# A linear-attention and adapter kernel: a new hand-written order of all instructions, an earlier gate for the stores, and a last slot finished in two halves

## The chip, the cores and the metric

The kernel runs on one core of one Trainium2 chip. The metric is device microseconds of one execution. A profiled execution has, beside its own time, a span: the time from the first to the last instruction of the program in the trace. The core has these engines, and each takes its instructions strictly from a list of its own: TensorE (PE, with its weight loads shown apart as PEld), VectorE (DVE), ScalarE (ACT), GpSimd (POOL) and SyncE (SP), which here only issues transfers.

## The reference, cut to what matters

```python
# q, k, v: (8, 8, 576, 64) float32: batch, heads, sequence, head dimension
r_q, r_k = relu(q), relu(k)
q_p = concat(r_q * cos_w, r_q * sin_w)        # cos_w, sin_w depend on the position alone
k_p = concat(r_k * cos_w, r_k * sin_w)
kv  = einsum('bhsf,bhsd->bhfd', k_p, v);  z = sum(k_p, axis=2)
x   = einsum('bhsf,bhfd->bhsd', q_p, kv) / (einsum('bhsf,bhf->bhs', q_p, z) + 1e-6)
x   = x.transpose(0, 2, 1, 3).reshape(4608, 512)

logits = x @ w_gate                           # 8 experts
top 2 of the logits, softmax over the two -> w
out = x + sum over the two experts e of  w_e * ((x @ A[e]) @ B[e])     # rank 16
```

The output is 4608 x 512 float32, 9.4 MB; q, k and v are 28 MB together.

## The kernel before, in words

**Batches and slots.** The eight batches are loaded one after another, each as three transfers, v, k and q, which also turn float32 into bf16 on the way (batch 0's v and k come as float32). The 4608 output rows are worked off in 36 slots of 128 rows. Nine slots belong to two batches; every ninth slot from 4 on is mixed, half its rows from each of the two. Slot n of 0 to 8 needs batches 0 and 1, 9 to 17 batches 2 and 3, and so on.

**One batch.** `vs` scales v by the cosine and by the sine of the position: 18 instructions (9 sequence parts, 2 tables), spread over ACT, POOL and, for the first batches, DVE. `rk` is the relu of k, `qc` of q, in two halves `qc,b,0` and `qc,b,1`, on DVE. `kv` is 72 small matmuls in three parts into the PSUM tile `big`; `kve` copies their sum to SBUF, in two halves.

**One slot.** `qt` transposes q on PE, `qe` multiplies by the tables (DVE). `nd` makes numerators and denominators on PE in the one PSUM tile `nd`; `re` is the reciprocal, `no` the quotient x (both DVE, both reading `nd`, so the next slot's `nd` waits for `no`). `xt` and `xe` transpose x by way of the PSUM tile `xz` and copy it, `za` multiplies it with the adapters' A and the gate's columns, `mx` takes the largest logits.

**One group of up to three slots** (`GROUPS`; the last one holds slot 35 alone). `nm` sums the two largest logits, `mk` marks the experts that are out, `tt` and `cb` make the sigmoid's argument, `sg` is the sigmoid (ACT), `zg` multiplies, `zt` transposes (into the other half of `xz`) and `ze` copies. A softmax over two logits is the sigmoid of their difference, so `tt` computes 2 * logit - sum, and `cb` pushes the others far down.

**Output of a slot.** `dx` adds x (turned into row order by a permutation matmul) and the adapters' product in a PSUM bank, `oe` copies it to one of 22 output buffers, `st` stores 256 KB by SP's queue.

**What sets the order.** Nothing is scheduled by a compiler: the string `ORDER` names every piece of work with its engine (`T` PE, `A` ACT, `V` DVE, `G` and `W` POOL, `S` SP) and its arguments, and each engine's list is the order in which its pieces stand there. An instruction waits for what it reads, and for the readers of what it overwrites; behind a waiting instruction its whole engine waits. `W` is a scaling on POOL that waits in addition for DVE's latest `vs`, `rk` or `qc`. `dm` are matmuls of ones without a use for the result, which keep PE running in waits; a further 36 stand at the start.

**The gate.** SP's list has, ahead of the first store, a tiny transfer `gate` that reads the q of batch 7 and so waits for its landing. The stores stand behind it:

```python
    def gate(e, b):
        e.dma_start(out=gone, in_=q_b[b % 5][0:1, 0, 0, 0:2])
```

Of the kernel before, what the change touches and what calls it, by code (L numbers as in the profile page):

```python
# [22 lines left out]
ldv,G,2,0 vs,A,0,0,1 vs,V,0,0,0 ldk,G,2,0 vs,V,0,1,0 vs,A,0,1,1 vs,V,0,3,0 vs,A,0,2,1 vs,V,0,3,1 ldq,G,2,0  # L23
vs,V,0,4,0 vs,A,0,2,0 vs,V,0,4,1 vs,A,0,5,0 ldv,G,3,0 vs,V,0,6,0 vs,V,0,6,1 vs,A,0,5,1 vs,V,0,7,1 vs,A,0,7,0
# [30 lines left out]
xt,T,17 oe,A,11 re,V,18 za,T,15 no,V,18 qt,T,20 ze,A,4 za,T,16 xe,A,17 dx,T,12,b0 qe,V,20 nd,T,19 oe,A,12
mx,V,15 mx,V,16 qc,V,5,0 xt,T,18 za,T,17 vs,W,6,0,0 vs,A,6,0,1 re,V,19 dx,T,13,b1 no,V,19 xe,A,18 vs,G,6,1,0
dx,T,14,b0 vs,A,6,3,0 mx,V,17 vs,G,6,1,1 rk,V,5,0 nd,T,20 oe,A,13 vs,W,6,2,0 xt,T,19 oe,A,14 qt,T,21 mk,V,5
nm,V,5 re,V,20 vs,G,6,2,1 xe,A,19 tt,V,5 no,V,20 kv,T,5,0 vs,G,6,3,1 vs,A,6,6,1 cb,V,5 kv,T,5,1 qe,V,21
vs,G,6,4,0 sg,A,5 vs,A,6,8,1 xt,T,20 vs,G,6,4,1 zg,V,5 kv,T,5,2 xe,A,20 vs,G,6,5,1 qc,V,5,1 nd,T,21 vs,W,6,5,0
kve,A,5,1 rk,V,6,0 zt,T,5 vs,W,6,6,0 za,T,18 kve,A,5,0 qt,T,22 za,T,19 ze,A,5 re,V,21 qt,T,23 qe,V,22 vs,G,6,7,0  # L60
dx,T,15,b0 vs,G,6,7,1 mx,V,18 mx,V,19 dx,T,17,b1 no,V,21 vs,G,6,8,0 za,T,20 qt,T,24 oe,A,15 qe,V,23 xt,T,21
nd,T,22 oe,A,17 mx,V,20 qe,V,24 xe,A,21 kv,T,6,0 mk,V,6 vs,G,7,0,1 vs,A,7,0,0 nm,V,6 re,V,22 qt,T,25 tt,V,6
no,V,22 vs,A,7,1,0 vs,G,7,2,0 kv,T,6,1 vs,A,7,1,1 vs,G,7,2,1 qt,T,26 cb,V,6 qe,V,25 sg,A,6 nd,T,23 vs,G,7,3,0
vs,A,7,3,1 zg,V,6 xt,T,22 vs,G,7,5,0 vs,A,7,4,0 kv,T,6,2 re,V,23 xe,A,22 vs,G,7,6,0 no,V,23 za,T,21 vs,G,7,8,0
kve,A,6,1 zt,T,6 mx,V,21 qe,V,26 nd,T,24 vs,G,7,8,1 ze,A,6 za,T,22 kve,A,6,0 qc,V,6,0 xt,T,23 mx,V,22 vs,A,7,4,1
re,V,24 dx,T,16,b0 no,V,24 xe,A,23 dx,T,18,b1 vs,A,7,5,1 qc,V,6,1 za,T,23 nd,T,25 oe,A,16 rk,V,7,0 gate,S,7
# [43 lines left out]
def kernel(ctx, tc, q, k, v, w_gate, A, Bw, out):  # L110
# [105 lines left out]
    def gate(e, b):  # L216

        e.dma_start(out=gone, in_=q_b[b % 5][0:1, 0, 0, 0:2])
# [273 lines left out]
```

## Time and profile before

| | |
|---|---|
| median of 3 runs | 108.87 us (108.86 to 109.73) |
| the profiled execution | 108.97 us |
| its span | 107.2 us |
| busy: PE, DVE, ACT, POOL | 91.7, 91.5, 83.0, 51.7 us |
| loads | 24 of q, k and v, the last one awaited until 75.93 us |
| stores | 36, first issued at 76.80 us |
| granted PE clock, mean | 0.999 |

In the profile, a line of a timeline has the start in us from the span's start, the duration in us, the engine (with a q behind it where its sequencer issues or waits), the line of the kernel, the operation, what it writes and reads, and a count where neighbours are merged; in brackets stands the engine's idle time just before, and what ended it. Two neighbours on one engine can overlap by some hundredths of a microsecond, because the next one starts while the last results are being written. A line of waits has the total in us, the number of times and the longest. A line of a stretch has its bounds and length, the busy time of PE, PEld, DVE, ACT and POOL with instruction counts, the granted clock, the busy share of the DMA engines and the GB/s.

### The profile page before, as it was taken

The page shows a single profiled execution, that of the slowest core. Times are in us where ns is not written, and L with a number is a line of the kernel's source. Part 1 is how long each engine was busy: PE and PEld are TensorE (multiplying, and loading weights), DVE is VectorE, ACT ScalarE, POOL GpSimd, SP SyncE. Part 2 cuts the span into 40 slices and gives each one's busy share as a digit, 9 for nine tenths or more (in the row PEclk, how much of TensorE's full clock was granted, in tenths as well). Part 3 has the DMA queues.
Part 4 walks back from the last instruction along what each step waited for, and adds up shares of the span by engine and source line. Part 5 has one row for each costly group of instructions (what it writes and reads, how often), then busy time and mean ns, then how long its engine had stood idle before and what let it go on. Part 6 is the DMA issues. An engine that isn't in the chain of part 4 may idle for free.

```text
span 107.2 us, 4004 instructions
## 1 busy us (share of the span) xinstructions
PE 91.7 (86%) x1605; PEld 66.1 (62%) x1618; DVE 91.5 (85%) x272; ACT 83.0 (77%) x182; POOL 51.7 (48%) x99
## 2 busy tenths in 40 slices
PE   4999379796987988999999989998998999998820
PEld 1344256574746867877877878785886687565300
DVE  5889389969999899998989998989999899986810
ACT  6956348968996995699899999589969676567730
POOL 6992033322993899699799399785000000000000
PEclk9999999999999999999999999999999999999999
DMA  2999999999999999999999999997088989989892
GB/s 35 368 345 293 203 224 233 207 208 208 206 207 210 208 207 209 207 209 207 208 208 208 212 202 208 207 208 131 1 323 308 381 299 385 359 332 382 323 358 95
DMA packets 19222, 25.56 MB, mean 238 GB/s; under 512 B 2180, under 2 KB 13444, under 8 KB 19204
## 3 DMA queue, kind: packets, MB, share of 16 engines
q0 software_dynamic: 11616, 12.98, 70.9%
q1 hardware_dynamic: 7060, 12.21, 32.1%
q8 instruction: 12, 0.20, 0.7%
q10 hardware_dynamic: 528, 0.13, 0.6%
q14 instruction: 6, 0.05, 0.1%
HBM read 28.85 MB, written 9.44 MB: 357 GB/s over the span
## 4 chain that ended last, share of the span: by engine, by line
DMA 43%; ACT 17%; PE 15%; DVE 10%; POOL 7%; issue 4%; POOLq 0%; ACTq 0%
DMA v<-in_v_dram 41%; ACT vs L239 6%; PE big L254 3%; ACT kvsb L271 3%; PE xz L345 3%; ACT xT L349 2%; DMA out_dram<-k0f 2%; ACT zgT L402 2%; DVE qT L293 2%; POOL vs L240 2%; DVE xt L334 2%; POOL q L197 2%; PE nd L320 2%; PE big L409 2%; PE za L354 1%
## 5 line engine op out<-in xcount | busy, mean ns | idle before, releaser
L240 POOL TENSOR_SCALAR vs<-v,tab 128x256 bf16<-128x256 bf16 x67 | 33.0, 509 | 4.3 <-DVE rden L329 1.9
L239 ACT ACTIVATE vs<-v,tab 128x256 bf16<-128x256 bf16 x57 | 25.6, 504 | 1.6 <-DMA v<-in_v_dram 1.5
L293 DVE TENSOR_TENSOR qT<-pq,tabq 128x1024 bf16<-128x1024 bf16 x36 | 24.1, 678 | 1.2 <-PE pq L285 1.1
L349 ACT COPY xT<-xz 128x512 bf16<-128x512 bf16 x34 | 19.9, 586 | 5.5 <-PE xz L345 5.0
L320 PE MATMUL nd<-kvsb,qT 128*128 128x130 bf16 (+1 forms) x256 | 19.1, 222 | 1.1 <-DVE qT L293 0.7
L339 DVE TENSOR_TENSOR xt<-nd,rden 128x512 bf16<-128x512 f32 x28 | 19.3, 688 | 0.5
L320 PEld LDWEIGHTS <-qT 128*128 128x128 bf16 (+1 forms) x256 | 13.7, 100 | 4.6 <-issue 3.1
L345 PE MATMUL xz<-ident,xt 128*128 128x128 bf16 x144 | 14.0, 220 | 1.7 <-ACT xT L349 0.6
L354 PE MATMUL za<-AW,xT 128*128 128x136 bf16 x144 | 14.3, 223 | 0.3 <-ACT xT L349 0.2
L254 PE MATMUL big<-vs,k 64*64 64x130 bf16 x576 | 12.0, 221 | 2.4 <-DVE k L247 2.1
L285 PE MATMUL pq<-ident,qq 128*128 128x128 bf16 x144 | 13.1, 220 | 0.3 <-DVE qT L293 0.2
L345 PEld LDWEIGHTS <-xt 128*128 128x128 bf16 x144 | 10.4, 114 | 3.9 <-issue 2.0
L354 PEld LDWEIGHTS <-xT 128*128 128x128 bf16 x144 | 9.9, 98 | 3.7 <-ACT xT L349 0.7
L409 PE MATMUL big<-xt,turn 128*128 128x512 bf16 x28 | 10.6, 379 | 1.5 <-ACT kvsb L271 0.5
L254 PEld LDWEIGHTS <-k 64*64 64x64 bf16 x576 | 8.9, 106 | 4.7 <-DVE k L247 2.7
L436 PE MATMUL nd<-ones 128*128 128x512 bf16 x36 | 9.5, 430 | 1.5 <-DVE eps_hi L437 1.5
L315 PE MATMUL nd<-eps_hi,ones 128*128 128x4 bf16 x56 | 9.5, 169 | 1.3 <-DVE xt L339 1.0
L285 PEld LDWEIGHTS <-qq 128*128 128x128 bf16 x144 | 9.0, 98 | 2.5 <-issue 0.7
L197 POOL DMA_DIRECT2D q<-in_q_dram x8 | 6.3, 787 | 8.2 <-DMA v<-in_v_dram 2.7
L271 ACT CAST kvsb<-big 64x520 bf16<-64x520 f32 x15 | 8.9, 593 | 1.5 <-PE big L254 1.3
L410 PE MATMUL big<-Ball,zgT 128*128 128x512 bf16 x25 | 9.5, 379 | 0.3
L278 DVE TENSOR_SCALAR qq<-q 128x1152 bf16<-128x1152 bf16 x16 | 8.1, 512 | 1.6 <-DMA q<-in_q_dram 1.6
(76 smaller groups left out, 142.1 us busy)
## 6 DMA issues: line engine op xcount, KB each, us to landing
q<-in_q_dram POOLq DMA_DIRECT2D x8, 576.0 KB, 22.7
v<-in_v_dram POOLq DMA_DIRECT2D x7, 576.0 KB, 22.5
k<-in_k_dram POOLq DMA_DIRECT2D x7, 576.0 KB, 22.6
out_dram<-k SPq DMA_DIRECT2D x10, 256.0 KB, 3.4
out_dram<-v0f SPq DMA_DIRECT2D x8, 256.0 KB, 3.4
out_dram<-k0f SPq DMA_DIRECT2D x8, 256.0 KB, 3.4
out_dram<-v SPq DMA_DIRECT2D x6, 256.0 KB, 3.3
v0f<-in_v_dram SPq DMA_DIRECT2D x1, 1152.0 KB, 5.8
```

What stands on the lines that cost most here:

```text
L239: return e.activation(dst, src, AF.Copy, bias=0.0, scale=t)
L240: return e.tensor_scalar(out=dst, in0=src, scalar1=t, scalar2=1.0, op0=ALU.mult, op1=ALU.mult)
L254: e.matmul(out=big[halves[g2], par, gp * 2 * W:(gp + 1) * 2 * W], lhsT=k_b[b][pr, 2 * gp + g2, s, :], rhs=vs_t[b % NV][pr, s, 2 * gp + g2, ...
L271: (e.copy if e is nc.scalar else e.tensor_copy)(dst, src)
L285: e.transpose(out=d[:, gp, :, jj, :], in_=q2_t[b % 3][:, gp, s].rearrange("p g d -> p (g d)"), identity=ident)
L293: e.tensor_tensor(out=qT_t[n % NQ], in0=src, in1=tab, op=ALU.mult)
L320: e.matmul(out=nd[pr, par, gp * 2 * W:(gp + 1) * 2 * W], lhsT=qT[:, i, gp * 2 + par, js], rhs=kv_t[b % 3][:, par, gp, i, :], start=False, ...
L339: e.tensor_tensor(out=x.rearrange("p (a t d) -> p t a d", t=2, d=D), in0=nds()[:, :, :, 0:D], in1=rd.rearrange("p (t a) -> p t a", t=2).to ...
L345: e.transpose(out=xz[:, c * 128:(c + 1) * 128], in_=x[:, c], identity=ident)
L349: (e.copy if e is nc.scalar else e.tensor_copy)(xT_t[n % 3], src)
L354: e.matmul(out=zs[:, i, :], lhsT=xT_t[n % 3][:, c, :], rhs=AW[:, c, :], start=(c == 0 and i == 0), stop=(c == DCH - 1), skip_group_check=True)
L409: e.matmul(out=d, lhsT=turn, rhs=x_t[n % NX], start=True, stop=False)
```

## The change

Four things change.

1. `ORDER` is rewritten from the second line on. The same pieces stand in another order, and some go to another engine: DVE gives up `cw` 1, one half of `kve` 0 and one `ze` (slots' groups 3 and 9 before, 8 after), and takes three more `vs` and `oe` 28; its two `xe` are those of slots 1 and 7 where they were 0 and 1. ACT has 60 `vs` where it had 65, POOL 69 where it had 67. There are 17 `dm` where there were 10. `rk` and `qc` of the late batches stand elsewhere: `qc,V,7,0` behind `no` 25 where it stood behind `no` 27.
2. The gate reads v of batch 7, and a second tiny transfer reads what the first one wrote. The stores stand behind both.
3. The last group, slot 35 alone, gets forms of its own: `nm` makes the negated sum, which goes into the sigmoid as its bias with a factor of 2 on the logits, so that `tt` and `cb` fall away; `mk` marks the experts that stay, and a new piece `zm` on DVE multiplies them into the products ahead of `zg`.
4. The last slot's `dx` writes two halves of 256 columns into two PSUM banks, `oe` copies one on ACT and one on DVE, and the two halves are stored by SP's and by ACT's queue.

The beginning and the end of the new order, and the other edits:

```diff
 ldv,S,0,0 pre,G start,A ldk,S,0,0 kz,V,0 ldw,S ldq,G,0,0 tq,A cols,V kz,V,1 ldv,G,1,0 kz,V,2 ldk,G,1,0 ldq,G,1,0
...
-vs,V,0,8,1 vs,A,0,8,0 rk,A,0,1 rk,V,0,0 kv,T,0,0 ldk,G,3,0 qc,V,0,0 kv,T,0,1 qc,V,0,1 kv,T,0,2 qt,T,0 kve,A,0,0
-qt,T,1 qe,V,0 kve,V,0,1 dm,T,n0 dm,T,n0 qt,T,2 cw,A,0 qe,V,1 nd,T,0 qe,V,2 qt,T,3 re,V,0 no,V,0 ldq,G,3,0
-vs,A,1,0,0 vs,V,1,6,1 vs,A,1,0,1 dm,T,b0 dm,T,b0 dm,T,b0 dm,T,b0 nd,T,1 vs,V,1,7,1 vs,W,1,2,0 vs,A,1,1,0 qe,V,3
-xt,T,0 vs,A,1,1,1 re,V,1 vs,A,1,2,1 xe,V,0 no,V,1 vs,A,1,3,0 dm,T,b0 dm,T,b0 dm,T,b0 za,T,0 vs,A,1,3,1 mx,V,0
-cw,V,1 nd,T,2 vs,A,1,4,0 ldv,G,4,0 rk,V,1,0 vs,A,1,5,1 xt,T,1 vs,A,1,5,0 re,V,2 xe,V,1 dm,T,b0 kv,T,1,0
-vs,A,1,4,1 no,V,2 vs,A,1,6,0 za,T,1 kv,T,1,1 vs,A,1,7,0 mx,V,1 nd,T,3 vs,A,1,8,0 vs,A,1,8,1 ldk,G,4,0 qc,V,1,0
...
+vs,V,0,8,0 vs,A,0,8,1 rk,A,0,1 rk,V,0,0 kv,T,0,0 ldk,G,3,0 qc,V,0,0 kv,T,0,1 qc,V,0,1 kv,T,0,2 qt,T,0 kve,A,0,1
+qt,T,1 qe,V,0 kve,A,0,0 qe,V,1 dm,T,n0 dm,T,n0 dm,T,n0 nd,T,0 cw,A,0 qt,T,2 qt,T,3 re,V,0 qe,V,2 no,V,0
+ldq,G,3,0 vs,A,1,1,1 vs,V,1,0,0 dm,T,b0 dm,T,b0 dm,T,b0 dm,T,b0 nd,T,1 vs,V,1,0,1 vs,A,1,2,0 vs,V,1,1,0
+vs,W,1,8,0 xt,T,0 vs,A,1,2,1 vs,V,1,3,0 vs,A,1,4,1 re,V,1 vs,A,1,5,0 vs,V,1,3,1 no,V,1 vs,A,1,4,0 vs,A,1,6,0
+qe,V,3 dm,T,b0 dm,T,b0 dm,T,b0 dm,T,b0 dm,T,b0 nd,T,2 vs,A,1,5,1 ldv,G,4,0 rk,V,1,0 vs,A,1,6,1 vs,A,1,7,0 re,V,2
+dm,T,b0 dm,T,b0 dm,T,b0 kv,T,1,0 vs,A,1,7,1 no,V,2 vs,A,1,8,1 kv,T,1,1 xe,A,0 nd,T,3 cw,A,1 xt,T,1 ldk,G,4,0
+qc,V,1,0 kv,T,1,2 re,V,3 xe,V,1 za,T,0 kve,A,1,1 no,V,3 xt,T,2 za,T,1 kve,A,1,0 qc,V,1,1 xe,A,2 mx,V,0 mx,V,1
+dm,T,q0 dm,T,q0 qt,T,4 qt,T,5 xt,T,3 qe,V,4 za,T,2 ldq,G,4,0 vs,A,2,0,0 mx,V,2 nd,T,4 vs,A,2,1,0 qe,V,5
...
-xt,T,35 mk,V,11 nm,V,11 dx,T,30,q1 tt,V,11 xe,A,35 cb,V,11 dx,T,31,b1 sg,A,11 dx,T,32,q0 oe,A,30 zg,V,11 oe,V,31
-za,T,35 oe,A,32 st,S,30 zt,T,11 mx,V,35 ze,A,11 mk,V,12 st,S,31 nm,V,12 dx,T,33,b0 tt,V,12 cb,V,12 st,S,32
-dx,T,34,q1 sg,A,12 oe,A,33 zg,V,12 oe,V,34 zt,T,12 st,S,33 ze,A,12 dx,T,35,b1 st,S,34 oe,A,35 st,S,35
+tt,V,11 xe,A,35 cb,V,11 dx,T,31,q0 sg,A,11 dx,T,32,b0 oe,A,30 zg,V,11 oe,V,31 zt,T,11 oe,A,32 st,S,30 za,T,35
+ze,A,11 mx,V,35 st,S,31 mk,V,12 nm,V,12 dx,T,33,b1 zm,V,12 st,S,32 sg,A,12 dx,T,34,q1 oe,A,33 zg,V,12 zt,T,12
+oe,V,34 st,S,33 ze,A,12 dx,T,35,q0,b0 st,S,34 oe,A,35,0 oe,V,35,1 st,S,35,0 st,A,35,1
 """
...
     def gate(e, b):
 
-        e.dma_start(out=gone, in_=q_b[b % 5][0:1, 0, 0, 0:2])
+        e.dma_start(out=gone, in_=v_b[b][0:1, 0, 0, 0:2])
+        e.dma_start(out=gone2, in_=gone)
...
     def nm(e, g):
         n = len(GROUPS[g])
+        if n == 1:
+
+            m8 = m8_t[g % 2][:, 0]
+            return e.tensor_scalar(out=ms_t[g % 2][:, 0:1], in0=m8[:, 0:1], scalar1=m8[:, 1:2], scalar2=-1.0,
+                                   op0=ALU.add, op1=ALU.mult)
...
     def mk(e, g):
         n = len(GROUPS[g])
+        if n == 1:
+            return e.tensor_scalar(out=mk_t[g % 2][:, 0], in0=zs[:, 0, ER:ZW], scalar1=m8_t[g % 2][:, 0, 1:2],
+                                   scalar2=None, op0=ALU.is_ge)
...
+    def zm(e, g):
+        e.tensor_tensor(out=zm_t, in0=zs[:, 0, 0:ER].rearrange("p (e r) -> p e r", e=E),
+                        in1=mk_t[g % 2][:, 0].to_broadcast([128, E, R]), op=ALU.mult)
...
     def sg(e, g):
         n = len(GROUPS[g])
+        if n == 1:
+            return e.activation(u_t[g % 2][:, 0], zs[:, 0, ER:ZW], AF.Sigmoid, bias=ms_t[g % 2][:, 0:1], scale=2.0)
...
     def zg(e, g):
         n = len(GROUPS[g])
+        if n == 1:
+            return e.tensor_tensor(out=zg_t[g % 2][:, 0], in0=zm_t, in1=u_t[g % 2][:, 0].to_broadcast([128, E, R]),
+                                   op=ALU.mult)
...
-    def dx(e, n, bank):
+    def dx(e, n, bank, bank2=None):
...
+        if bank2:
+
+            bank_of[n, 0], bank_of[n, 1] = h = [banks[k][:, 0:DM // 2] for k in (bank, bank2)]
+            for i in range(2):
+                e.matmul(out=h[i], lhsT=turn, rhs=x_t[n % NX][:, i * DM // 2:(i + 1) * DM // 2], start=True, stop=False)
+            for i in range(2):
+                e.matmul(out=h[i], lhsT=zgT_t[g % 3][:, n - GROUPS[g][0], :], rhs=Ball[:, i * DM // 2:(i + 1) * DM // 2],
+                         start=False, stop=True)
+            return
...
-    def oe(e, n):
-        (e.copy if e is nc.scalar else e.tensor_copy)(o_t[n % NO], bank_of[n])
-
-    def st(e, n):
+    def oe(e, n, h=None):
+        d, s = (o_t[n % NO], bank_of[n]) if h is None else (o_t[n % NO][:, h * DM // 2:(h + 1) * DM // 2], bank_of[n, h])
+        (e.copy if e is nc.scalar else e.tensor_copy)(d, s)
+
+    def st(e, n, h=None):
...
+        c = slice(0, DM) if h is None else slice(h * DM // 2, (h + 1) * DM // 2)
+        e.dma_start(out=dst[:, :, c].rearrange("j r d -> r j d"), in_=o_t[n % NO][:, c])
```

More of the change, by code (lines that the diff above doesn't have):

```diff
@@ L62 @@
[L62 to L66, printed above, removed]
@@ new lines @@
+dx,T,12,b1 mx,V,16 re,V,18 xe,A,17 vs,G,5,8,1 no,V,18 dx,T,13,b0 za,T,17 rk,V,5,0 nd,T,19 oe,A,12 vs,W,6,0,0
+oe,A,13 xt,T,18 mx,V,17 qt,T,20 mk,V,5 nm,V,5 vs,G,6,0,1 qt,T,21 re,V,19 xe,A,18 tt,V,5 kv,T,5,0 no,V,19
+vs,G,6,1,0 vs,A,6,2,0 cb,V,5 vs,G,6,1,1 kv,T,5,1 vs,A,6,2,1 qe,V,20 xt,T,19 sg,A,5 vs,G,6,3,0 vs,A,6,3,1
+kv,T,5,2 zg,V,5 vs,G,6,4,0 xe,A,19 nd,T,20 qe,V,21 vs,G,6,5,0 kve,A,5,1 zt,T,5 qc,V,5,1 vs,G,6,4,1 za,T,18
+kve,A,5,0 re,V,20 qt,T,22 mx,V,18 vs,W,6,5,1 no,V,20 ze,A,5 za,T,19 dx,T,14,b0 vs,A,6,6,0 vs,G,6,6,1 mx,V,19
@@ L180 @@
     gone = sb("gone", [1, 2])
+    gone2 = sb("gone2", [1, 2])
     AW = sb("AW", [128, DCH, ZW])
```

97 lines of the change are left out of this document (48 added, 49 removed).

## The prediction

> **What bounds the kernel now.** I read first the stretches of the span by engine, then what DVE waits for, then the timelines of DVE and of SP (the queue of the stores), and last the end of the run.
>
> ```profile
> span 107.2 us, 4004 instructions
> 80.00:90.00 10.00, 9.43 (x176) 7.04 (x176) 9.49 (x31) 7.18 (x15) 0.00 (x0) 1.00 0.92 339
> ...
> DVE m L360 <- PE za L354: 1.0, 4, 0.3
> ...
> DVE qT L293 <- PE pq L285: 0.7, 2, 0.4
> DVE zg L388 <- ACT u L384: 0.7, 2, 0.3
> DVE rden L329 <- PE nd L320: 0.2, 1, 0.2
> ...
> 23.53 0.46 DVE L278 TENSOR_SCALAR qq<-q 128x1152 bf16<-128x1152 bf16 x1 [0.96 <-DMA q<-in_q_dram]
> ```
>
> The row of the stretch from 80 to 90 us has its length, then PE, weight load, DVE, ACT and POOL busy: DVE 9.49 of 10 us, PE 9.43. PE's matmuls overlap and their ends are modelled, so I take DVE as the bound. The four waits are all that DVE shows between 23.5 and 96.6 us beside one landing, that of the second batch's q at 23.53 (last row): 2.6 us in 73. So up to 23.5 us the loads set the pace, then the length of DVE's list does, and from 96.6 us (`no` of slot 35) a chain through all engines.
>
> ```profile
> 75.93 0.75 SPq L218 DMA_DIRECT2D gone<-q  x1
> 76.80 2.60 SPq L419 DMA_DIRECT2D out_dram<-v0f  x4
> ...
> 102.41 1.40 SPq L419 DMA_DIRECT2D out_dram<-v  x2
> 70.00:72.80 2.80, 2.69 (x77) 2.18 (x75) 2.45 (x8) 2.78 (x8) 2.72 (x7) 1.00 1.21 208
> 72.80:75.70 2.90, 2.63 (x33) 1.88 (x33) 2.87 (x8) 2.88 (x7) 0.93 (x3) 1.00 0.53 91
> 75.70:77.50 1.80, 1.80 (x30) 1.48 (x28) 1.68 (x8) 1.80 (x5) 0.00 (x0) 1.00 0.00 0
> ```
>
> The stores go out from 76.80 to 102.41. The last two leave SP together, behind the last copies. The three stretches end in clock, DMA share and GB/s: loads at full rate, the last load's bytes ending, nothing at all. So DMA has a hole here, but the end does not hang on it: the last store waits for its copy, not for the queue.
>
> **The change, part by part.** *Stores let go by the last v.* The gate now waits for v of batch 7, two loads earlier, and a second tiny copy waits for the first.
>
> ```profile
> 70.08 0.48 POOL L240 TENSOR_SCALAR vs<-v,tab 128x256 bf16<-128x256 bf16 x1 [1.16 <-DMA v<-in_v_dram]
> 76.44 0.69 DVE L339 TENSOR_TENSOR xt<-nd,rden 128x512 bf16<-128x512 f32 x1
> DMA to landing us min/median/max: 2.4/3.4/4.4
> ```
>
> That v is there at 70.0. The trace shows no landing for a tiny copy. Lower bound: its issue alone, 0.75 us; upper: the longest store, 4.4. I take the shortest store, 2.4, the nearest thing to a transfer without size. Then `gone2` goes out at 72.4 and the first store 0.75 later, at 73.2 (71.5 to 75.2), some 3.6 us before today. By the Trainium skill ("DMA: Bandwidth & Descriptors", Anatomy of one DMA) a transfer has a fixed cost of about 2.0 us, by which it would be 72.8; no run so far shows a copy this small. Worth to the end: nothing by itself, because the last store waits for compute; it hides behind DVE. Without this cover, with compute over a microsecond faster, the stores' backlog would have become the bound, so it keeps that gain open. Queued behind the two waits on SP are only stores.
>
> *DVE's list behind the landing of q of batch 1.* Ahead of it DVE gives up the second half of `kve` 0, `cw` 1, `xe` 0 and 1 and `mx` 0 and 1, for three more scalings `vs`: idle time there, priced nothing, as 23.53 is the landing's. It costs if the stretch then lasts past 23.53. Behind it, up to `no` 35, the list gains two `xe` (slots 1 and 7), two `mx` and `oe` 28, and loses one of two `ze`.
>
> ```profile
> L349 DVE COPY xT<-xz 128x512 bf16<-128x512 bf16 x2 | 0.8, 386 | 0.0
> L413 DVE COPY k<-big 128x512 f32<-128x512 f32 x1 | 0.7, 680 | 0.0
> L402 DVE COPY zgT<-xz 128x384 bf16<-128x384 bf16 x2 | 1.2, 580 | 0.0
> L360 DVE MAX8 m<-za 128x8 f32<-128x8 f32 x36 | 5.3, 164 | 1.3 <-PE za L354 1.3
> ...
> 94.53 0.20 DVE L329 RECIPROCAL rden<-nd 128x8 f32<-128x8 f32 x1
> 94.65 0.19 DVE L373 SCALAR_TENSOR_TENSOR za<-za,ms 128x24 f32<-128x24 f32 x1
> 94.76 0.69 DVE L334 TENSOR_TENSOR xt<-nd,rden 128x512 bf16<-128x512 f32 x1
> 95.37 0.18 DVE L379 SCALAR_TENSOR_TENSOR za<-mk,za 128x24 f32<-128x24 f32 x1
> 95.89 0.56 DVE L388 TENSOR_TENSOR zg<-za,u 128x384 bf16<-128x384 f32 x1 [0.34 <-ACT u L384]
> 96.36 0.20 DVE L329 RECIPROCAL rden<-nd 128x8 f32<-128x8 f32 x1
> 96.59 0.69 DVE L334 TENSOR_TENSOR xt<-nd,rden 128x512 bf16<-128x512 f32 x1
> ```
>
> An instruction starts about 0.08 us before the one ahead has ended (94.76 + 0.69 = 95.45, the next starts at 95.37), so I price each 0.08 under its duration: 2 x 0.31 + 2 x 0.08 + 0.60 - 0.50 = **+0.9 us**.
>
> *Neighbours on DVE.* The rows show something else: a reciprocal followed by something independent takes 0.12 us to the next start (94.53 to 94.65), one followed by its own `no` takes 0.23 (96.36 to 96.59). An instruction that needs the result just ahead of it pays about 0.11. I counted the neighbours in both orders between the landing and `no` 35: `re` straight before its `no`, 18 times now, 12 in the new order; `nm` straight before `tt`, 3 and 1; `cb` straight before `zg`, 1 and 0.
>
> ```profile
> 97.89 0.15 DVE L364 TENSOR_REDUCE ms<-m 128x2 f32<-128x4 f32 x1
> 98.07 0.18 DVE L373 SCALAR_TENSOR_TENSOR za<-za,ms 128x16 f32<-128x16 f32 x1
> ```
>
> `nm` before its `tt` takes 0.18, so I give it the same 0.11 too much; `cb` before `zg` stands 0.52 (95.37 to 95.89, the wait for the sigmoid), where `tt` with a stranger behind it takes 0.11 (94.65 to 94.76). So 6 x 0.11 + 2 x 0.11 + 0.41 = **-1.3 us**. Bounds: 0, if each such pause only covers a wait that shows up next, and -1.3. The Trainium skill ("VectorE: DVE Perf Modes", The DRAIN you can't avoid) has every DVE instruction wait until the pipe is empty, with or without a semaphore between. By that rule neighbours cost nothing and this term is 0. The rows 0.12 and 0.23 for the same reciprocal speak against it.
>
> *DVE's waits on PE.*
>
> ```profile
> 66.41 0.69 DVE L293 TENSOR_TENSOR qT<-pq,tabq 128x1024 bf16<-128x1024 bf16 x1 [0.35 <-PE pq L285]
> ```
>
> This is `qe` 22, the longest of them: now only a reciprocal stands between its transposes and it, in the new order `mx` 18, `no` 20 and `mx` 19. The others change places in both directions. I take **-0.3 us**; bounds -2 (nearly all go) and +3 (below).
>
> *PE and ACT.*
>
> ```profile
> L265 PE MATMUL big<-ones 128*128 128x512 bf16 x7 | 1.8, 379 | 0.0
> ```
>
> Seven more of these dummies, all ahead of slot 4, while PE waits for the loads and for DVE: nothing; 2.7 us at most if none of that wait is left. ACT gives up five `vs` and one and a half `oe`, takes a `cw`, a `kve` and a `ze`. ACT is not the bound (7.2 busy of 10 from 80 to 90 us): nothing.
>
> *The last slot.*
>
> ```profile
> 100.12 0.16 DVE L360 MAX8 m<-za 128x8 f32<-128x8 f32 x1
> 100.40 0.14 DVE L364 TENSOR_REDUCE ms<-m 128x1 f32<-128x2 f32 x1
> 100.58 0.17 DVE L373 SCALAR_TENSOR_TENSOR za<-za,ms 128x8 f32<-128x8 f32 x1
> 101.05 0.18 ACT L384 ACTIVATE u<-za 128x8 f32<-128x8 f32 x1 [0.41 <-DVE za L379]
> 101.26 0.29 DVE L388 TENSOR_TENSOR zg<-za,u 128x128 bf16<-128x128 f32 x1 [0.30 <-ACT u L384]
> 101.13 0.58 ACT L413 COPY k<-big 128x512 f32<-128x512 f32 x1
> 101.87 0.30 ACT L402 COPY zgT<-xz 128x128 bf16<-128x128 bf16 x1 [0.16 <-PE xz L394]
> 102.66 0.58 ACT L413 COPY v<-big 128x512 f32<-128x512 f32 x1 [0.48 <-PE big L410]
> ```
>
> Today 3.1 us from `mx` 35 to the end of the copy (103.24). The bias form lets the sigmoid follow `nm`: `tt` and `cb`, between 100.58 and the sigmoid at 101.05, fall out, 0.4 us. `zm` (0.29, like the `zg` row) fits into DVE's 0.30 wait. Against it: `za` 35 now stands behind `zt` 11 on PE, about +0.2; and ACT does `oe` 33 first, from 101.13 to 101.71, so `ze` 12 cannot start before 101.65, 0.2 ahead of today. Then two half copies, on ACT and DVE at once: 0.30 to 0.58 each, I take 0.4. End of the copies about 102.8: **-0.4 us** (-0.2 to -0.7). The halves leave by two queues, SP and ACT, but SP has the store of slot 34 just ahead as today: **-0.2 us** (0 to -0.4).
>
> **Sum:** 0.9 - 1.3 - 0.3 - 0.4 - 0.2 = -1.3 us. The profiled execution took 108.97 us, 1.77 beside its span; the median of the runs is 0.1 lower. So 107.67, on the median's scale **107.6**.
>
> **The rivals.** (1) *Neighbours cost nothing* (the skill's DRAIN rule above gives the same): -1.3 becomes 0, 108.9. The double value of the reciprocal speaks against it; for it, that a list as full as this may just wait elsewhere.
>
> (2) *New waits, slower.* Six reciprocals of the new order (slots 0, 10, 19, 28, 29, 32) have under 0.3 us of DVE work between the place of their `nd` and their own, where two do now. An `nd` is two groups like this one, so 0.4 to 0.8 us:
>
> ```profile
> 62.28 0.40 PE L320 MATMUL nd<-kvsb,qT 128*128 128x130 bf16 x4
> ```
>
> If PE reaches each of them only when its place in the list says, DVE stands 0.5 us six times, 3 us that nothing gives back: 107.6 + 3 = 110.6. It decides as soon as PE runs later than DVE by more than the work between. Against: an `nd` needs the `no` before it, and between that `no` and `re` lie 0.6 us or more in all but two slots, as today; the reciprocal's wait is 0.2 us in all now.
>
> (3) *Stores meet the last loads.* If the gate costs only its issues, stores start at 71.5. The loads' last bytes end at about 74.1 today, if 1.21 is a load's full share: 72.8 plus 0.53 / 1.21 of 2.9 us. A store's bytes follow its issue by 0.7 us or more (76.80, none before 77.5), so 1.9 us of loads are left, and sharing evenly they take 1.9 longer. `qc` 7 moves from behind `no` 27 to behind `no` 25 and one `qe`: about 77.1 (76.44 plus 0.7), against 75.9 when the gate saw that q. 1.2 us are free, 0.7 paid: 108.3. The Trainium skill ("DMA: Bandwidth & Descriptors", Queues, rings and completion order) has each DMA engine take turns between queues by packets; that is this even sharing, and here the stretch without bytes after 75.7 says that by 73.2 little is left to share.
>
> (4) *The new order also waits less:* 2 us of the 2.6 go, 105.6.
>
> **How the numbers follow.** Forecast 0.48 (its own range 106.8 to 108.2), rival 1 0.15, rival 2 0.22 (109.0 to 111.5), rival 3 0.05, rival 4 0.10. One per cent, about what a measurement of this kernel tells from no change, is 1.09 us: faster means below 107.78. Of the forecast 0.40 lies there, with rival 4 that is 0.50; slower (above 109.96) is 0.16 of rival 2 and a rest of rival 1, 0.18; 0.32 stays within. The range leaves out a tenth at each end: 105.7 to 110.3.
>
> **What would show it.** Right: DVE's `no` 35 near 96.1 with DVE's waits after 23.5 us no longer than now, start-to-start of 0.12 in more reciprocals, first store near 73, last copy near 102.3, q of batch 7 awaited by nobody. Wrong: `rden` or `m` waits of several microseconds, `qc` 7 waiting for its load, or DVE passing the landing at 23.5 with work left over.

## The result: no gain, 0.4% slower

The changed kernel takes 109.38 us (median of 22 runs), the kernel before 108.88 (22 runs): ratio 1.0043, interval 1.0026 to 1.0060. The forecast was 107.6. The profiled executions took 109.46 and 108.97 us; their spans, 107.4 and 107.2, differ by 0.2. The other 0.3 lies beside the span (a run's time less its span): 2.06 against 1.77 us here, a median of 2.01 with up to 3.16 in the 22 runs, against 1.73 to 1.85 in 112 runs of the kernel before (spans are kept to 0.1 us, so each of these is known to about 0.05). One of the runs below, at a granted clock of 0.67, took 127.63 us, and the ratios leave it out.

The same four stretches of the span as before, then DVE's waits from 23.5 to 96.9 us:

```profile
80.00:90.00 10.00, 9.58 (x224) 7.17 (x224) 9.46 (x30) 6.68 (x13) 0.00 (x0) 1.00 0.92 338
70.00:72.80 2.80, 2.80 (x85) 2.31 (x86) 2.68 (x9) 2.13 (x6) 2.48 (x6) 1.00 1.22 208
72.80:75.70 2.90, 2.62 (x49) 1.89 (x47) 2.87 (x8) 2.86 (x7) 2.90 (x7) 1.00 0.56 97
75.70:77.50 1.80, 1.80 (x29) 1.62 (x28) 1.73 (x7) 1.80 (x4) 0.28 (x1) 1.00 0.83 307
```

```profile
DVE qq L282 <- DMA q<-in_q_dram: 1.2, 1, 1.2
DVE m L364 <- PE za L358: 0.5, 2, 0.3
DVE qT L297 <- PE pq L289: 0.4, 2, 0.2
DVE rden L333 <- PE nd L313: 0.3, 1, 0.3
DVE zg L409 <- ACT u L402: 0.2, 1, 0.2
DVE rden L333 <- PE nd L324: 0.2, 1, 0.2
```

DVE is as full as it was (9.46 of 10 us) and waits 1.6 us beside the landing where it waited 2.6. The hole in the DMA after 75.7 us is filled. Both were forecast, and the end did not come earlier. (The view lists a wait only from 0.15 us on.)

DVE's timeline: the landing of q of batch 1, a stretch around `no` 33, slot 35 and the last slot.

```profile
23.69 0.46 DVE L282 TENSOR_SCALAR qq<-q 128x1152 bf16<-128x1152 bf16 x1 [1.24 <-DMA q<-in_q_dram]
...
92.14 0.20 DVE L333 RECIPROCAL rden<-nd 128x8 f32<-128x8 f32 x1
92.50 0.69 DVE L297 TENSOR_TENSOR qT<-pq,tabq 128x1024 bf16<-128x1024 bf16 x1 [0.16 <-PE pq L289]
93.11 0.68 DVE L338 TENSOR_TENSOR xt<-nd,rden 128x512 bf16<-128x512 f32 x1
...
96.66 0.20 DVE L333 RECIPROCAL rden<-nd 128x8 f32<-128x8 f32 x1
96.89 0.69 DVE L338 TENSOR_TENSOR xt<-nd,rden 128x512 bf16<-128x512 f32 x1
...
100.31 0.17 DVE L364 MAX8 m<-za 128x8 f32<-128x8 f32 x1
100.66 0.20 DVE L371 TENSOR_SCALAR ms<-m 128x1 f32<-128x1 f32 x1
100.79 0.29 DVE L384 TENSOR_TENSOR zm<-za,mk 128x128 f32<-128x128 f32 x1
101.49 0.29 DVE L407 TENSOR_TENSOR zg<-zm,u 128x128 bf16<-128x128 f32 x1 [0.41 <-ACT u L401]
101.71 0.69 DVE L444 COPY v<-pq 128x512 f32<-128x512 f32 x1
102.95 0.42 DVE L444 COPY v<-big 128x256 f32<-128x256 f32 x1 [0.55 <-PE big L436]
```

`no` 35 starts at 96.89 (forecast 96.1; 96.59 before): 73.20 us behind the landing, 73.06 before. From `no` 35 to the end of the span it is 10.5 us, 10.6 before. So the miss of 1.8 us splits, on the two profiled executions, into four: DVE's stretch between the landing and `no` 35 grew by 0.14 us where 0.7 less was forecast (0.84), the landing came 0.16 later, the end saved 0.1 instead of 0.6 (0.5), and 0.3 lies beside the span. Four kernels further down have the changed kernel's order of DVE up to `no` 35 (`old_slot`, `one_queue`, `sg_first`, `gate_q`): their profiled stretches are 72.95 to 73.06 long, and those of `before_slot` and `before_gate`, with the order of before, 72.88 and 72.86. So a growth of 0.14 can't be told from no change; that the 0.7 did not come is clear.

### The profile page after: what moved, and what is told of

It reads as the page before. It is cut to its first block, busy times and chain, and to the rows that moved or that the text cites. A ratio compares the mean times of both kernels' runs of the same rounds, so it can differ in the third digit from the quotient of the medians.

```text
span 107.4 us, 4030 instructions
## 1 busy us (share of the span) xinstructions
PE 93.0 (87%) x1613; PEld 66.3 (62%) x1627; DVE 91.8 (85%) x273; ACT 82.9 (77%) x179; POOL 52.2 (49%) x101
## 4 chain that ended last, share of the span: by engine, by line
PE 40%; DMA 19%; ACT 19%; DVE 9%; POOL 4%; issue 4%; POOLq 0%; DVEq 0%; ACTq 0%
DMA v<-in_v_dram 19%; ACT vs L243 7%; PE nd L324 6%; PE za L358 6%; PE big L258 5%; PE xz L349 5%; PE big L439 5%; PE big L440 3%; PE pq L289 3%; ACT kvsb L275 3%; ACT zgT L423 3%; ACT xT L353 2%; DVE xt L343 2%; PE xz L415 2%; PE nd L313 2%
## 5 line engine op out<-in xcount | busy, mean ns | idle before, releaser
L243 ACT ACTIVATE vs<-v,tab 128x256 bf16<-128x256 bf16 x52 | 23.4, 503 | 1.8 <-DMA v<-in_v_dram 1.7
L275 ACT CAST kvsb<-big 64x520 bf16<-64x520 f32 x16 | 9.5, 594 | 2.8 <-PE big L258 2.5
L468 PE MATMUL nd<-ones 128*128 128x512 bf16 x36 | 10.2, 453 | 1.5 <-DVE eps_hi L469 1.5
L440 PE MATMUL big<-Ball,zgT 128*128 128x512 bf16 x23 | 8.7, 379 | 0.5 <-ACT zgT L423 0.4
```

Source lines behind the costliest of these rows:

```text
L243: return e.activation(dst, src, AF.Copy, bias=0.0, scale=t)
L275: (e.copy if e is nc.scalar else e.tensor_copy)(dst, src)
```

## The experiments

Each is compared with the kernel before in runs on the same chip. The rows below the first come from four chips; the kernel before has a median span of 107.2 on three of them and of 107.1 on the fourth (`fill_only`, `before_gate`, `dm17`, `tail_um`), so differences of 0.1 us between rows tell little. The column "over 1.9" counts runs with more than 1.9 us beside the span.

| kernel | median us | ratio, interval | span, median | over 1.9 |
|---|---|---|---|---|
| changed | 109.38 | 1.0043 (1.0026-1.0060) | 107.3 | 17 of 22 |
| `adjacent` | 110.49 | 1.0121 (1.0096-1.0146) | 108.5 | 3 of 6 |
| `fill_first` | 109.93 | 1.0090 (1.0059-1.0121) | 108.05 | 3 of 8 |
| `fill_only` | 109.49 | 1.0068 (1.0040-1.0095) | 107.4 | 9 of 12 |
| `oe28` | 109.20 | 1.0013 (0.9996-1.0031) | 107.4 | 1 of 12 |
| `before_slot` | 108.84 | 0.9986 (0.9969-1.0002) | 107.1 | 0 of 12 |
| `old_slot` | 109.08 | 1.0019 (0.9998-1.0039) | 107.2 | 4 of 12 |
| `one_queue` | 109.23 | 1.0029 (1.0004-1.0055) | 107.2 | 6 of 12 |
| `sg_first` | 109.25 | 1.0024 (1.0002-1.0046) | 107.25 | 9 of 12 |
| `gate_q` | 109.45 | 1.0064 (1.0033-1.0095) | 107.65 | 4 of 12 |
| `before_gate` | 109.02 | 0.9998 (0.9981-1.0015) | 107.2 | 0 of 12 |
| `dm10` | 110.33 | 1.0114 (1.0083-1.0145) | 108.55 | 0 of 6 |
| `dm17` | 109.12 | 1.0020 (1.0004-1.0036) | 107.35 | 3 of 12 |
| `dm24` | 110.43 | 1.0119 (1.0091-1.0147) | 108.45 | 3 of 6 |
| `tail_um` | 108.79 | 0.9994 (0.9974-1.0013) | 107.0 | 0 of 12 |
| `best` | 108.84 | 0.9982 (0.9963-1.0002) | 107.05 | 0 of 12 |

**Neighbours.** The theory: each reciprocal straight ahead of its own `no` costs 0.11 us of the end. The rival: the pause only stands in for a wait. `adjacent` is the changed kernel with all 36 pairs side by side:

```
-re,V,1 vs,A,1,5,0 vs,V,1,3,1 no,V,1        (23 slots like this)
+vs,A,1,5,0 vs,V,1,3,1 re,V,1 no,V,1
```

> The changed kernel (109.4 us, span 107.4) with one difference: every reciprocal stands directly ahead of its own `no` on DVE, in all 36 slots instead of 13. Nothing is added or removed. By the forecast's term a reciprocal with its own `no` behind it costs 0.11 us more than one with a stranger behind it, and DVE's list sets the end: 23 more such pairs, 2.5 us, so a span near 109.9 and about 111.9 us. The rival is that the pauses only take the place of waits for PE, because the reciprocal is DVE's wait for `nd` and `no` lets the next `nd` go: then the waits shrink by what the pauses cost and the span stays within 0.4 us of 107.4.

The span grew by 1.2 us (108.5 against 107.3), between the two: on average 0.05 us for each of the 23 pairs, half the price. DVE's waits beside the landing, and one pair, of `adjacent`:

```profile
DVE m L361 <- PE za L355: 0.3, 1, 0.3
DVE qT L294 <- PE pq L286: 0.2, 1, 0.2
```

```profile
93.73 0.20 DVE L330 RECIPROCAL rden<-nd 128x8 f32<-128x8 f32 x1
93.96 0.69 DVE L335 TENSOR_TENSOR xt<-nd,rden 128x512 bf16<-128x512 f32 x1
```

The pair still steps 0.23, so the single pause was read rightly; but the reciprocal's waits for `nd` (0.5 us in the changed kernel) are gone, and those for `za` and `pq` fell from 0.9 to 0.5. Part of the pauses is paid back by waits that no longer happen.

The half is an average of two stretches, as `no` of slots 14 and 35 shows. First `no` 14 of the changed kernel (its `no` 35, at 96.89, stands in the section on the result), then both of `adjacent`:

```profile
51.75 0.69 DVE L343 TENSOR_TENSOR xt<-nd,rden 128x512 bf16<-128x512 f32 x1
```

```profile
51.68 0.69 DVE L340 TENSOR_TENSOR xt<-nd,rden 128x512 bf16<-128x512 f32 x1
...
97.76 0.69 DVE L335 TENSOR_TENSOR xt<-nd,rden 128x512 bf16<-128x512 f32 x1
```

From the landing (23.69 and 23.61) to `no` 14 ten more pairs cost nothing: 28.06 against 28.07 us (0.3 at most against the four kernels with this order). From there to `no` 35 eleven more cost 0.9 us (45.14 against 46.08), 0.08 each. Of the changed kernel's seven listed waits in the whole stretch, five lie ahead of `no` 14, 1.2 of the 1.6 us. So a pause was free where DVE had waits, and cost about three quarters of its price where it had few. The other direction shows in the changed kernel at 92.14: behind the reciprocal stands a stranger, `qe` 35, and waits 0.16 us for PE instead.

**The work behind the landing.** The forecast priced the work that DVE has more behind the landing at +0.9 us. `fill_first` puts the first two slots' copies and maxima back ahead of the landing and `xe` 7 on ACT; `fill_only` leaves `xe` 7 on DVE; `oe28` moves one output copy to ACT:

```
-rk,V,1,0 ... re,V,2 ... xe,A,0 ... qc,V,1,0 ... xe,V,1 za,T,0 ... za,T,1 ... mx,V,0 mx,V,1
+xe,V,0 ... za,T,0 xt,T,1 rk,V,1,0 mx,V,0 re,V,2 xe,V,1 ... za,T,1 ... mx,V,1 ... qc,V,1,0
-xe,V,7                       (fill_first alone)
+xe,A,7
```

```
-oe,V,28 sg,A,10
+sg,A,10 oe,A,28
```

> The changed kernel with the work of the first two slots back ahead of the landings: the copies `xe` 0 and 1 on DVE, with `za` 0 and 1 on PE and `mx` 0 and 1, stand ahead of `qc` 1 instead of behind it, and `xe` 7 goes back to ACT. In the changed kernel DVE stood still for 1.19 us before the landing of k of batch 1 and for 1.24 us before that of its q. If the forecast's +0.9 us for this part was right, the list behind the landing gets shorter by 2 x 0.31 + 2 x 0.08 = 0.8 us: span near 106.6, about 108.6 us. The rival: what DVE gains here it loses again further on in waits for PE, since slot 32 had caught up with the kernel before anyway: span 107.4 as now.

> `fill_first` without its second edit: `xe` 7 stays on DVE as in the changed kernel, `xe` 0 and 1, `za` 0 and 1, `mx` 0 and 1 stand ahead of the landings. In `fill_first` slot 9 came 0.9 us late because `xe` 7 stood behind both halves of `kve` 2 on ACT and PE waited for it. If that is all, this kernel has the span of the changed one, 107.4, and the fill is worth nothing; if the forecast's price of work behind the landing holds, 0.47 us less, 106.9. If the 0.9 us comes from somewhere else, it stays at 108.0.

> The changed kernel with one output copy, `oe` 28, back on ACT (behind the sigmoid of group 10) instead of on DVE between `cb` 10 and `zg` 10. The forecast priced it at 0.60 us of DVE's list. If DVE's list still sets the end there, `no` 35 comes at 96.3 instead of 96.9 and the span is 106.8. The rival: the fill's work, priced the same way, was worth nothing, and here `xe` 34 and `xe` 35 on ACT come 0.4 us later behind the copy, so that `mx` 33 and 34 wait for PE: span 107.2 to 107.5.

`fill_first` came out 0.75 us longer instead of 0.8 shorter. Its own second edit did that: on ACT, `xe` 7 stands behind `kve` 2, PE waits for it, and DVE for PE. ACT, then PE, then DVE of `fill_first`:

```profile
37.92 0.57 ACT L350 COPY xT<-xz 128x512 bf16<-128x512 bf16 x1
```

```profile
38.54 0.33 PE L412 MATMUL xz<-ident,zg 128*128 128x128 bf16 x3 [0.70 <-ACT xT L350]
```

```profile
40.49 0.17 DVE L361 MAX8 m<-za 128x8 f32<-128x8 f32 x1 [0.99 <-PE za L355]
```

Without it, `fill_only` has the changed kernel's span to 0.1 us: work that was priced at 0.47 (0.36, as `re` 2 now stands at its own `no`) is worth nothing. `oe28` has 107.4, so nothing of its 0.60 reached the end either. But it is not a clean test of the 0.60: without `oe` 28 between them, `cb` 10 stands straight ahead of `zg` 10 again, the pause that the forecast priced at 0.41. DVE behind the landing in `fill_only`, then the landing and the stretch around `no` 35 in `oe28`:

```profile
25.70 0.69 DVE L294 TENSOR_TENSOR qT<-pq,tabq 128x1024 bf16<-128x1024 bf16 x1 [0.32 <-PE pq L286]
26.57 0.17 DVE L361 MAX8 m<-za 128x8 f32<-128x8 f32 x1 [0.18 <-PE za L355]
```

```profile
23.57 0.46 DVE L279 TENSOR_SCALAR qq<-q 128x1152 bf16<-128x1152 bf16 x1 [1.24 <-DMA q<-in_q_dram]
...
95.66 0.56 DVE L406 TENSOR_TENSOR zg<-za,u 128x384 bf16<-128x384 f32 x1 [0.35 <-ACT u L399]
96.37 0.69 DVE L335 TENSOR_TENSOR xt<-nd,rden 128x512 bf16<-128x512 f32 x1
97.43 0.25 DVE L361 MAX8 m<-za 128x8 f32<-128x8 f32 x2 [0.37 <-PE za L355]
```

What DVE no longer does it waits for: 0.5 us in `fill_only` (0.24 at that place in the changed kernel), 0.72 in `oe28` (none). In `oe28` the 0.35 is the pause of `cb` 10 come back. Even so its `no` 35 came 72.80 us behind the landing, 0.15 to 0.4 ahead of the five kernels with that order; that gain was lost behind `no` 35, where `mx` 33 waits 0.37 us for PE. So these prices were durations of DVE's list, and the list alone did not set the pace.

**The last slot.** `before_slot` is the order and gate of before with the new slot; `old_slot` the new order and gate with the old one; `one_queue` sends both halves by SP; `sg_first` writes the sigmoid ahead of `zm`; `tail_um`, on the order of before, drops `mk` and `zm` and masks the sigmoid's result.

```
before_slot: -tt,V,12 cb,V,12 ... dx,T,35,b1 ... oe,A,35 st,S,35
             +zm,V,12 ... dx,T,35,b1,q0 ... oe,A,35,0 oe,V,35,1 st,S,35,0 st,A,35,1
one_queue:   -st,A,35,1     +st,S,35,1
sg_first:    -zm,V,12 st,S,32 sg,A,12     +sg,A,12 zm,V,12 st,S,32
tail_um:     +e.scalar_tensor_tensor(out=u, in0=logits, scalar=second largest, in1=u, op0=is_ge, op1=mult)
```

> The kernel before with its own order and gate, but with the last slot's new forms: bias sigmoid, two half copies, two queues. Theory A: the time beside the span rises to 2.1 to 2.5 us and the sum to 109.2; the span stays at 107.2, as the sigmoid then waits for the new product ahead of it on DVE and the half on DVE ends no earlier than the whole copy did. Theory B: no more than 108.9, with 1.8 beside the span. What I forecast of this part, 0.6 us less, would be 108.3.

> The changed kernel with its new order and its new gate, but the last slot done as before: sigmoid after two more DVE steps, one copy on ACT, one store on SP's queue. The changed kernel takes 109.38 us against 108.88, and its profiled execution has 2.06 us beside the span against 1.77. Theory A, the last slot's second store on ACT's queue is what costs outside the span: 108.9 here, with 1.8 us beside the span. Theory B, what lies outside the span comes with the order or the gate's second transfer: 109.3 or more here. For the span both expect 107.4, as the last slot's new forms moved the end of the last copy by no more than 0.1 us.

> The changed kernel with both halves of the last slot stored by SP's queue, one behind the other, where one of them went by ACT's. Theory A (ACT's queue costs outside the span): 1.8 us beside the span; the second half's store is issued about 0.65 us after the first, at 104.2, so the span grows to 107.9; sum 109.7, or 109.4 if the shorter list of queues at the end gives something back. Theory B: the time beside the span stays at 2.1 to 2.5 and the sum is 110.

> The changed kernel with the last slot's sigmoid written ahead of `zm` instead of behind it. In the changed kernel `nm` ended at 100.87 and the sigmoid started at 101.19, behind the end of `zm` at 101.07. If the order between the two readers of the PSUM bank holds up the sigmoid, it starts 0.2 to 0.3 us earlier, but then `zm` waits for the sigmoid instead (0.27 us) and the product `zg` comes no earlier: span 107.2 to 107.5. If the two don't hold each other up, the end comes 0.2 to 0.3 us earlier, 107.1 to 107.2. Either way the forecast's 0.4 us for the bias form does not come back in full.

> The kernel before (order and gate) with another form of the last slot: the sigmoid with its bias straight behind `nm`, no mask `mk` and no `zm` ahead of it; the mask is put on the sigmoid's result by one small instruction (logits not under the second largest, times u), then the plain product `zg`; two output halves on two queues as in the change. `before_slot` had a span of 107.05 with sigmoid and `zm` one behind the other. If the sigmoid can start 0.12 us behind `nm`, and `nm` comes 0.2 us earlier without `mk` ahead, the product starts 0.1 to 0.3 us earlier: span 106.8 to 107.0. If the small instruction behind the sigmoid costs what it saves, 107.05.

The new slot is worth 0.1 us of span in the old order (`before_slot`, 107.1 against 107.2) and nothing in the new one (`old_slot`, 107.2, `one_queue`, 107.2, changed, 107.3). `before_slot` on ACT, then `sg_first` on ACT and on DVE:

```profile
100.95 0.27 ACT L399 ACTIVATE u<-za,ms 128x8 f32<-128x8 f32 x1 [0.32 <-DVE zm L382]
```

```profile
100.91 0.27 ACT L401 ACTIVATE u<-za,ms 128x8 f32<-128x8 f32 x1 [0.25 <-DVE ms L371]
```

```profile
101.21 0.29 DVE L384 TENSOR_TENSOR zm<-za,mk 128x128 f32<-128x128 f32 x1 [0.42 <-ACT u L401]
101.53 0.29 DVE L407 TENSOR_TENSOR zg<-zm,u 128x128 bf16<-128x128 f32 x1
```

Sigmoid and `zm` never run side by side: whichever is written second waits for the first. Both read the bank of `za` and neither writes it, so this is a wait that the rule of `ORDER` as told above (an instruction waits for what it reads, and for the readers of what it overwrites) does not have. In the changed kernel the sigmoid started at 101.19, behind the end of `zm` at 101.08, not behind `nm` at 100.86. The Trainium skill ("PSUM — Partial Sum Buffer", PSUM bank collisions raise a hardware error) says that the compiler's scheduler adds a dependency between any two instructions on different engines that touch the same part of a bank, "reads and writes alike", ACT and DVE included, and that the hardware does not stall by itself. The two orders above agree with such a dependency; who put it into this program, which no compiler schedules, is not shown. `tail_um` moves the mask behind the sigmoid: 107.0, the same as `before_slot` to 0.1.

The halves lose time on SP. ACT's copy and SP's last store in the changed kernel:

```profile
102.78 0.37 ACT L444 COPY v<-pq 128x256 f32<-128x256 f32 x1 [0.38 <-PE pq L436]
```

```profile
103.63 0.54 SPq L451 DMA_DIRECT2D out_dram<-v  x1
```

The first half was ready at 103.15 and went out 0.48 later, behind the store of slot 34, which itself went at 102.98. In the kernel before the last store went at 103.27, 0.03 behind its copy.

**The gate.** `gate_q` is the changed kernel with the old gate, `before_gate` the kernel before with the new one.

```
-e.dma_start(out=gone, in_=v_b[b][0:1, 0, 0, 0:2])       (before_gate: + and -  exchanged)
-e.dma_start(out=gone2, in_=gone)
+e.dma_start(out=gone, in_=q_b[b % 5][0:1, 0, 0, 0:2])
```

> The changed kernel with the gate of before: one tiny transfer that waits for q of batch 7, so that stores begin at about 76.8 us and not at 74.7. If the earlier stores carry nothing (the last stores wait for their copies), the same as the changed kernel, 109.4 within 0.2. If the second tiny transfer costs outside the span, 109.0. If stores were the bound behind slot 27, slower by up to 2 us, 111.

> The kernel before with the new gate alone: the stores wait for v of batch 7 and one tiny copy more, not for its q. Forecast: nothing, since the last store waits for its copy and not for the queue: span 107.2, 108.9 us. In the new order, the old gate made 5 of 12 runs 0.5 to 1.0 us longer; if that is the stores' own backlog it must be a property of any order and the new gate gains up to 0.2 us here at most, because no run before shows a second, longer span.

SP's timeline of the changed kernel, then SP's waits:

```profile
69.42 0.75 SPq L221 DMA_DIRECT2D gone<-v  x1
74.00 0.59 SPq L222 DMA_DIRECT2D gone<-gone  x1
74.72 2.66 SPq L451 DMA_DIRECT2D out_dram<-v0f  x4
...
102.98 1.19 SPq L451 DMA_DIRECT2D out_dram<-v  x2
```

```profile
SPq L222 <- DMA gone<-v: 3.8, 1, 3.8
```

In the old order the new gate does nothing to the median, as forecast. In the new order the old gate made 5 of 12 spans 107.9 to 108.4 and left the others at 107.3 to 107.8. The profiled run is one of the short ones, so what those five waited for is not shown. Against the expectation of `before_gate`, longer spans are no property of the new order alone: the kernel before, with the old gate, has 18 of 112 at 107.5 to 108.1, and `before_gate` none of 12 above 107.4. Twelve runs are too few to say that the new gate removes them.

The tiny copy let go at 74.00, as the loads' bytes were running out: 191 GB/s from 73.0 to 73.5 us, 141 in the next half microsecond, 101 in the one behind it. In `before_gate` it let go at 73.68, in the same way. Whether it waited for the loads is not shown.

**The dummies.** `dm10` is the changed kernel with 10 dummy matmuls as before; `dm17` and `dm24` are the kernel before with 17 and 24.

```
dm10: -dm,T,n0  -dm,T,b0 dm,T,b0  -dm,T,b0 dm,T,b0  -dm,T,q0 dm,T,q0
dm17: +the same seven      dm24: +fourteen, the further seven at the last three places
```

> The changed kernel with 10 dummy matmuls in the fill, as before, instead of 17. The forecast put them at nothing. The new order's runs take 1.73 to 3.16 us beside the span (median 2.0) where the order before takes 1.73 to 1.84. If the seven dummies cause that (more load on PE early), it goes back to 1.8 for all runs and the time to about 109.2; if not, some runs still lie above 1.9. The span: unchanged at 107.4 if the dummies cover idle time, up to 0.5 shorter if they hold up `nd` 2 and `kv` 1, longer if PE's clock falls without them.

> The kernel before with 17 dummy matmuls in the fill instead of 10, at the places where the changed kernel has them. Every kernel with 17 dummies so far had runs with 1.9 to 3.2 us beside the span, whatever its slot or gate; every kernel with 10 (the kernel before, `before_slot`, `dm10`) stayed at 1.72 to 1.84. If the dummies cause it, some of these runs exceed 1.9 us beside the span. If the order causes it, all stay below 1.85. The span, 107.2 before: the changed kernel lost 1.2 us of span when its seven were taken out, so if that is worth as much in any order, 106.0; if it belongs to that order alone, 107.2.

> The kernel before with 24 dummy matmuls in the fill instead of 10 (17 gave 1.73 to 2.06 us beside the span, 3 of 12 runs above 1.9). If dummies cause what lies beside the span, it is now more and more often, over half of the runs above 1.9 and some at 2.5 or more as in the new order. If it was the order, it stays at about what 17 gave. The span: 107.2 with 10, 107.35 with 17, here 107.5 to 108.5, since seven more of 0.22 us stand on PE in the fill.

In the old order, seven more cost 0.25 us of span (107.35 against 107.1 on that chip) and fourteen 1.25: PE is not idle enough for them (in `dm24`, `no` 4 starts at 29.32 where it started at 27.68). In the new order, taking them out made it 1.2 us longer. The profiled `dm10` (107.9, the shortest of six) is 0.2 ahead of the changed kernel at slot 4, and goes from 0.15 ahead to 0.8 behind between `no` 8 and `no` 9. ACT, then PE, then DVE of `dm10`, then PE of the changed kernel at the same place:

```profile
36.27 1.20 ACT L272 CAST kvsb<-big 64x520 bf16<-64x520 f32 x2
37.37 0.90 ACT L240 ACTIVATE vs<-v,tab 128x256 bf16<-128x256 bf16 x2
38.17 0.57 ACT L420 COPY zgT<-xz 128x384 bf16<-128x384 bf16 x1
```

```profile
38.78 0.38 PE L436 MATMUL big<-xt,turn 128*128 128x512 bf16 x1 [1.13 <-ACT zgT L420]
```

```profile
40.39 0.17 DVE L361 MAX8 m<-za 128x8 f32<-128x8 f32 x1 [1.26 <-PE za L355]
```

```profile
37.67 0.38 PE L439 MATMUL big<-xt,turn 128*128 128x512 bf16 x1
```

`dx` 2 needs the bank that `kve` 2 read out, done at 37.47; it starts at 38.78, just behind a later copy that it does not use. In the changed kernel it followed `kve` 2 at once. Why it was let go late is open, and so is the rest of the 1.2 us, which this shortest run does not have.

Beside the span: with 10 dummies no run of the table is over 1.9, with 17 in the old order 3 of 12 (at most 2.06), with 24 3 of 6 (2.43). So in the old order more dummies bring it about. They are not all of it: with the same 17, the new order has it in 17 of 22 runs, and `oe28`, one copy apart from it, in 1 of 12. The kernels with this order ran on different chips, and no run separates chip from order. What it is stays open.

**A version from all this.** `best` has the old order and gate, `tail_um`'s slot, and four pairs taken apart.

```
-qc,V,1,0 xt,T,2 re,V,3     -cb,V,2 kv,T,3,2 re,V,11     -mx,V,22 vs,A,7,4,1 re,V,24     -cb,V,9 st,S,24 re,V,32
+re,V,3 qc,V,1,0 xt,T,2     +re,V,11 cb,V,2 kv,T,3,2     +re,V,24 mx,V,22 vs,A,7,4,1     +re,V,32 cb,V,9 st,S,24
```

> The kernel before with the last slot of `tail_um` (span 107.0) and four of the nineteen pairs of a reciprocal and its `no` taken apart, those four where PE had delivered long enough ahead: `re` 3 ahead of the landing, `re` 11 and 32 ahead of `cb` 2 and 9, `re` 24 ahead of `mx` 22. In the other fifteen PE had ended within 0.2 us of the reciprocal or the instruction ahead lasts longer than the room, so the pause there only stands in for a wait. At 0.05 us for each pair, as 23 more pairs cost in `adjacent`, 0.2 us: span 106.8, ratio 0.996 to 0.997. If the four also only covered waits that show up next: 107.0.

0.9982 (0.9963 to 1.0002): 107.05, no better than `tail_um`'s 107.0. DVE's waits in it from 23.3 us on:

```profile
DVE rden L328 <- PE nd L319: 1.8, 5, 0.9
DVE m L359 <- PE za L353: 1.0, 4, 0.3
```

The reciprocal waited 0.2 us in the kernel before. Here it waits 1.8: 0.9 once, where `re` 3 took over the wait for the landing, and 0.9 in four others. The gains of the four pairs went there. No version here is shown to beat the kernel before.

## Why the prediction was wrong

- **Neighbours, -1.3: the step that failed.** The single pause was right, but its price was taken to the end in full. I gave the bound 0 ("if each such pause only covers a wait that shows up next") and chose the other end. `adjacent` measures half on average, by which the six pairs would be worth about 0.3 us instead of 0.66. By place it is less: ahead of slot 14, where pauses were free in `adjacent`, the pairs went from 8 to 1, and behind it, where they cost, from 10 to 11. That the order of before behaves in the same way is an inference; `best`, which takes four pairs out of it, gained nothing. The pause at `cb` 10 did go, and comes back as 0.35 us in `oe28`; for `nm` no run separates it. The rule of the Trainium skill that made this rival 1 ("VectorE: DVE Perf Modes", The DRAIN you can't avoid) would have `adjacent` at no cost. The 1.2 us speaks against that; the section itself adds that a next instruction that is not held starts earlier. Rival 1's 108.9 was the nearest of the times given, and its mechanism, that such a list waits elsewhere, holds ahead of slot 14 only.
- **DVE's list, +0.9: right sum, wrong bound.** Moving 0.47 or 0.60 of it away changed the span by 0.1 at most (the 0.60 with `cb`'s pause coming back). Together these two show that "DVE is the bound" was only half true: in some stretches PE and DVE hold each other up. The prediction's own rows said so: PE 9.43 and DVE 9.49 busy of 10. PE's timeline of before shows `nd` of slot 35:

```profile
95.86 0.18 PE L302 MATMUL nd<-eps_hi,ones 64*128 64x4 bf16 x2
95.90 0.40 PE L309 MATMUL nd<-kvsb,qT 64*128 64x65 bf16 x16
```

  It ended at 96.30 (a modelled end), its reciprocal started at 96.36: no wait is listed, yet a reciprocal more than 0.06 earlier would have waited.
- **Waits on PE, -0.3:** on PE they fell by 0.5 (1.9 to 1.4), on ACT by 0.5 (0.7 to 0.2, with the 0.34 ahead of `zg` 10 that the prediction counts under neighbours), and the stretch did not get shorter by it. These parts do not close: +0.9 of work, -1.0 of listed waits and -0.66 at the reciprocals make -0.8, and +0.14 was measured. On DVE's timelines, the listed waits left out, the steps from a reciprocal's start to the next start did fall by 0.74 us in all, but the steps of the six `rk` grew by 0.31, of the 14 `qc` by 0.25 and of the 32 `no` by 0.23. So the saved pauses came back in pieces too short to be listed; what lengthens those steps stays open.
- **Last slot and halves, -0.6: mis-sized, 0.1.** The step "the bias form lets the sigmoid follow `nm`" is what failed: it follows `zm`. The half copies took 0.37 and 0.42 us as forecast (0.4), but the second half's matmul came behind the first, and its copy ended at 103.37, while the first half's store stood behind that of slot 34.
- **Gate, nothing:** right for the old order, by `before_gate`. The tiny copy was forecast at 2.4 us and kept SP until 74.00; the first store went at 74.72, in the range 71.5 to 75.2 and past the 73.2. The Trainium skill's 2.0 us ("DMA: Bandwidth & Descriptors", Anatomy of one DMA), which that section fits to transfers issued by POOL, would have given 72.8; the trace of this one, issued by SP, does not agree. That the cover is needed in the new order was said for a faster kernel; `gate_q` shows it 0.35 us dearer without one.
- **Dummies, nothing:** wrong in both orders, +0.25 in the old and, in the new, 1.2 us longer without them.
- **Rivals 2 and 3** did not happen: the reciprocals wait 0.5 us in all, and `qc` 7 waited for no load.
- **Not thought of:** time beside the span, 0.3 of the 1.8 us.

## What to carry to other kernels

Before an edit of one engine's list is priced, look in the other engine's timeline at how long its result had been ready: where PE ends 0.06 us ahead of DVE's read, most of a tenth saved on DVE turns into a wait. Then price the edit by stretch: the same pause was free where the engine had waits left and cost most of its length where it had few. A bound of 0 with such rows behind it is the value to take, not the far end. And two engines' reads of one PSUM bank came one behind the other here, so a chain that is cut short but gets a second reader saves less than its removed steps.

## What the runs showed of the hardware that was not expected

- A transfer of a few bytes, issued at 69.42 while the loads run at 208 GB/s, let the next one go only at 74.00, as those loads were ending: 4.6 us, where whole 256 KB stores took 2.4 to 4.4.
- `dx` 2 in `dm10` started 1.3 us after the copy whose bank it needs had ended, and 0.04 us after another one; the same matmul in the changed kernel took 0.05 us. The store of slot 34 went out at 102.98 in the changed kernel though its copy on DVE (from 101.71, 0.69 us) had ended at 102.40 and SP had been free since 102.5. Neither is explained.
- The time beside the span is not a constant of a program: 1.73 to 3.16 us from run to run for one kernel, 1.73 to 1.85 for another.
